# Layer A: two kinds of third score rounds in one PSUM tile, engine orders fixed by keys, products dealt anew

## The chip, the cores and the metric

The kernel runs on one core of a Trainium2 chip. The metric is the device time of one execution in microseconds (us). TensorE is called PE, VectorE DVE, ScalarE ACT, GpSimd POOL and SyncE SP, as in the profile.

## The reference

Four layers, A B A B, act on 2048 tokens of width 640, each as x = x + layer(layernorm(x)). Layer A is attention in 4 segments of 512 tokens with a memory that is carried from segment to segment; 32 heads of 20 columns:

```python
for s in range(N):                      # 4 segments
    logits = jnp.einsum('bhqd,bhkd->bhqk', qs, ks) * scale + mask   # causal
    p = _softmax(logits, axis=-1)
    a_dot = jnp.einsum('bhqk,bhkd->bhqd', p, vs)
    pq = phi(qs)                        # where(t > 0, t + 1, exp(t))
    a_mem = einsum(pq, M) / (einsum(pq, z)[..., None] + 1e-06)
    outs.append(g * a_mem + (1.0 - g) * a_dot)
    pk = phi(ks)
    M, z = M + einsum(pk, vs), z + sum(pk)
return o @ wo
```

Layer B is a recurrent one with 64 steps. The change does not touch it.

## The kernel before

The full kernel builds layer A, layer B, layer A and layer B one after the other. The first layer A reads x as bf16 from the input, the second reads fp32 rows from DRAM.

Layer A works on groups of 4 heads: 8 groups (G = 0 to 7) in each of 4 segments (n = 0 to 3), so g = 8n + G runs from 0 to 31, with two more turns of the loop to drain. A group has two halves, each of which takes one pair of heads. A half has two visits, and after each visit comes one of four slots (0 to 3) with other products.

In a visit two kinds of scores are made. The scores S have the queries on the partitions: only their row maxima are needed (`s_mask` adds the causal mask by a product, `s_mm` multiplies, `s_max` takes maxima on DVE). The turned scores T have the keys on the partitions; the maximum is already added into the queries (`negmax_rows`, `q_with_max`, tile q2), so that `t_round` multiplies and `t_exp` takes the exponential on ACT and then clears the upper triangle on POOL (a select). T runs three halves behind S. Each kind has three rounds for a pair: round 0 is 1024 elements to a partition (two heads with 512 columns), round 1 is 1024 and round 2 is 512. The maxima of round 1 are two instructions, of 768 and 256 elements. "S2" is the third round of S, "exp0" the exponential of the first round of T, and so on; a prime (S2', exp0') marks the second half of a group.

A round has one PSUM tile of two banks, from the pool `psx` with three buffers; `pg` has two buffers of one bank for all other products. Both are rings: a tile takes the buffer of the tile three (or two) places before it and waits until that one has been read. Before, a half takes six tiles, (S0, T0, S2) and (T1, S1, T2), and each visit reuses the buffers of the visit before it.

The other products of a group, by their tiles: QP and qT (the queries of the next group, `proj_q`), EQ, rq and phiq (phi of the queries), KV with Kn and vaug (keys and values, `proj_kv`, in two parts KV0 and KV1), KT and kT (turned keys, `k_turn`), EK and phik (`phi_k`; POOL clips EK between them, called EKm), NUM, nsb, rd and am (the memory's part, `state_num`), UP, upm, MZ and MZb (the memory's update, `state_up`), PV and osb (`pv`), rl, adn and Onat (`norm`). In segment 0 there is no NUM, EQ or phiq, in segment 3 no EK, phik or UP. The layernorm of the next segment is dealt out by `seg_step`: xt is loaded by `seg_load`, `seg_norm` takes statistics on DVE, a power on POOL and xn on DVE, and `seg_tr` turns xn on PE (tps) and copies it to xnT on ACT. The output of the segment before is dealt out by `filler`: `out_stage_a` loads xr and turns Onat (otps, oT), `out_stage_b` multiplies with wo (YP0 and YP1, one for each half of the columns), adds xr (xnew0 and xnew1 on DVE), stores the rows, makes a bf16 copy on POOL (xnb) and stores that. xnew has one buffer of its own in the first layer A, and is the tile xr (two buffers) in the second.

What sets the order: in layer A only PE runs in the order of the code (`_OrdNC` chains each instruction to the one before on its engine, `engines=("tensor",)`). The order on DVE, ACT and POOL is chosen when the program is built, by the scheduler of the language. On the chip each engine runs its own queue in order. Most of layer A's PE instructions carry L101 in the profile, the line of that helper.

Before, G = 2 to 5 of segments 1 to 3 hold an output tile each, and the four layernorm tiles stand in G = 0, 1, 6 and 6. The first layer A also loads layer B's resident weights, 1 MB at a time, from ACT's queue (`load_B_resident`, G = 0 to 4), each behind a small copy on POOL that waits for kT.

Of the kernel before, what the change touches and what calls it, by code (L numbers as in the profile page):

```python
# [18 lines left out]
F32 = mybir.dt.float32  # L19
# [9 lines left out]
D = 640  # L29
# [91 lines left out]

class AWeights:
    pass

# [36 lines left out]
def layer_A(nc, tc, C, W, x_src, x_dst, src_is_bf16, nseg=4, out_bf16=False, xb_dst=None, load_w=None, side_loads=None):  # L161
    SC = 1.0 / math.sqrt(20.0)
    nc_raw = nc
    nc = _OrdNC(tc, nc_raw, engines=("tensor",))
    NGR = 8 * nseg
    KOFF = (0, 640, 1024, 512)
    assert not out_bf16
    with ExitStack() as ctx:
# [65 lines left out]
        def seg_norm(n_, tt):  # L234
            d = SEG[n_]
            xt = d["xt"][tt]
            xn = pxn.tile([128, D], BF16, name="a_xn")
            layernorm_tile(nc, sml, C, xt[:, 0:D], xn[:], "a_ln")
            d["xn"][tt] = xn

        def seg_tr(n_, tt):
            d = SEG[n_]
            if "xnT" not in d:
                d["xnT"] = pxT.tile([128, NCH, 512], BF16, name="a_xnT", tag="xnT")
            xn = d["xn"][tt]
            tps = pg.tile([128, NCH, 128], BF16, name="a_tps", tag="pg")
            for c in range(NCH):
                nc.tensor.transpose(tps[:, c, :], xn[:, 128 * c:128 * c + 128], C.identb[:])
            nc.scalar.copy(d["xnT"][:, :, 128 * tt:128 * tt + 128], tps[:])

        def out_stage_a(n_, tt):
            d = SEG[n_]
            r0 = n_ * 512 + tt * 128
            xr = wkl.tile([128, D], BF16 if src_is_bf16 else F32, name="a_xr")
            nc.sync.dma_start(xr[:], x_src[r0:r0 + 128, :])
            oT = wkl.tile([128, NCH, 128], BF16, name="a_oT")
            d["xr"][tt], d["oT"][tt] = xr, oT
            tps = pg.tile([128, NCH, 128], BF16, name="a_otps", tag="pg")
            for c in range(NCH):
                nc.tensor.transpose(tps[:, c, :], d["Onat"][:, tt, 128 * c:128 * c + 128], C.identb[:])  # L260
            nc.scalar.copy(oT[:], tps[:])

        def out_stage_b(n_, tt, halves=(0, 1)):
# [6 lines left out]
            for half in halves:  # L270
                YP = pg.tile([128, 320], F32, name="a_YP", tag="pg")
                for c in range(NCH):
                    nc.tensor.matmul(YP[:], lhsT=oT[:, c, :], rhs=W.wo[:, c, 320 * half:320 * half + 320],
                                     start=(c == 0), stop=(c == NCH - 1))
                nc.vector.tensor_tensor(out=xnew[:, 320 * half:320 * half + 320], in0=YP[:], in1=xr[:, 320 * half:320 * half + 320], op=ALU.add)
# [4 lines left out]
            nc.gpsimd.tensor_copy(xnb[:], xnew[:])  # L280
# [4 lines left out]
        def proj_q(g):  # L285
# [8 lines left out]
            nc.scalar.copy(qT[:], QP[:])  # L294
            s_["qT"] = qT
            if n >= 1:
                EQ = w1.tile([128, 512], BF16, name="a_EQ")
                nc.scalar.activation(out=EQ[:], in_=QP[:], func=ACT.Exp)
                rq = w1.tile([128, 512], BF16, name="a_rq")
                nc.vector.tensor_scalar(out=rq[:], in0=qT[:], scalar1=0.0, scalar2=None, op0=ALU.max)  # L300
                phiq = wk.tile([128, 512], BF16, name="a_phiq")
                nc.vector.scalar_tensor_tensor(out=phiq[:], in0=EQ[:], scalar=1.0, in1=rq[:], op0=ALU.min, op1=ALU.add)
                s_["phiq"] = phiq

        def proj_kv(g, hf):
# [8 lines left out]
            for dst, o in ((Kn[g % 2], 0), (vaug[g % 4], 80)):  # L314
                nc.scalar.copy(dst[:, 2 * hf:2 * hf + 2, :, 0:20], KV[:, :, o:o + 80].rearrange("p t (j s) -> p t j s", s=20))
            GS[g]["va"] = vaug[g % 4]

        def k_turn(g):
# [4 lines left out]
            nc.scalar.copy(kT[:], KT_[:].rearrange("p t k -> p (t k)"))  # L323
            GS[g]["kT"] = kT

        def phi_k(g):
# [5 lines left out]
            nc.scalar.activation(out=EK[:], in_=KNv, func=ACT.Exp)  # L332
            nc.gpsimd.tensor_scalar(out=EK[:], in0=EK[:], scalar1=1.0, scalar2=0.0, op0=ALU.min, op1=ALU.max)
            pk = phik[g % 2]
            nc.vector.scalar_tensor_tensor(out=pk[:, :, :, 0:20], in0=KNv, scalar=0.0, in1=EK[:], op0=ALU.max, op1=ALU.add)
            GS[g]["pk"] = pk

        def state_num(g):
            n, G = divmod(g, 8)
            s_ = GS[g]  # L340
            if n >= 1:
# [5 lines left out]
                nc.scalar.copy(nsb[:], NUM[:, :, :, 0:21])  # L347
                rd = sm.tile([128, 4, 4], F32, name="a_rd", tag="rd")
                nc.vector.tensor_tensor(out=rd[:], in0=nsb[:, :, :, 20], in1=epsc[:].rearrange("p (a b) -> p a b", a=4), op=ALU.add)
                nc.vector.reciprocal(out=rd[:], in_=rd[:])  # L350
                nc.vector.tensor_tensor(out=rd[:], in0=rd[:], in1=W.g[:, 4 * G:4 * G + 4].unsqueeze(1).to_broadcast([128, 4, 4]), op=ALU.mult)
                am = up.tile([128, 4, 4, 20], F32, name="a_am", tag="am")
                nc.gpsimd.tensor_tensor(out=am[:], in0=nsb[:, :, :, 0:20], in1=rd[:].unsqueeze(3).to_broadcast([128, 4, 4, 20]), op=ALU.mult)
                s_["am"] = am

        def state_up(g):
            n, G = divmod(g, 8)
            s_ = GS[g]
            if n <= nseg - 2:
# [6 lines left out]
                nc.vector.tensor_tensor(out=upm[:], in0=UP[:], in1=C.bdmask[:], op=ALU.mult)  # L366
                nc.gpsimd.tensor_tensor(out=MZ32[:, G, :], in0=MZ32[:, G, :], in1=upm[:], op=ALU.add)
                nc.gpsimd.tensor_copy(MZb[:, G, :], MZ32[:, G, :])
# [27 lines left out]
        def s_max(p, r, X):  # L396
            g, pr = divmod(p, 2)
            nm = GS[g]["nm"]
            for qc, o, w_ in S_SPAN[r][2]:
                nc.vector.tensor_reduce(out=nm[:, qc, 2 * pr:2 * pr + 2], in_=X[:, :, o:o + w_], axis=AX.X, op=ALU.max, negate=True)  # L400

        def negmax_rows(g):
            nm, N_ = GS[g]["nm"], NM[g % 2]
            nc.gpsimd.tensor_copy(N_[:, :, :, 20], nm[:])
            nc.gpsimd.tensor_tensor(out=N_[:, :, :, 21], in0=nm[:], in1=N_[:, :, :, 20], op=ALU.subtract)

        def q_with_max(g):
# [8 lines left out]
            nc.scalar.copy(q2[:], Q2[:])  # L416
# [5 lines left out]
        def t_round(p, r, Y):  # L422
# [7 lines left out]
            for n_, (kc, o, w_) in enumerate(parts):  # L430
                for e in range(2):
                    j = 2 * pr + e
                    rows = slice(32 * j, 32 * j + 32)
                    nc.tensor.matmul(Y[:, e, o:o + w_], lhsT=kT[rows, 128 * kc:128 * kc + 128], rhs=q2[rows, 128 * kc:512],
                                     start=True, stop=True, tile_position=(32 * j, 0), skip_group_check=True)

        def t_exp(p, r, Y):
# [4 lines left out]
            nc.scalar.activation(out=PT[:, :, b:b + width], in_=Y[:, :, 0:width], func=ACT.Exp, scale=SC)  # L442
            dv = PT[:, :, b:b + 128 * diag].rearrange("p e (a q) -> p e a q", q=128)
            nc.gpsimd.affine_select(out=dv, in_=dv, pattern=[[0, 2], [0, diag], [1, 128]], compare_op=ALU.is_ge,  # L444
                                    fill=0.0, base=0, channel_multiplier=-1)

        def pv(g):
# [11 lines left out]
            nc.scalar.copy(osb[:], PV[:, :, :, 0:21])  # L459
            s_["osb"] = osb  # L460

        def norm(g):
# [6 lines left out]
            nc.vector.reciprocal(out=rl[:], in_=osb[:, :, :, 20])  # L469
            nc.vector.tensor_tensor(out=rl[:], in0=rl[:], in1=W.omg[:, 4 * G:4 * G + 4].unsqueeze(1).to_broadcast([128, 4, 4]), op=ALU.mult)  # L470
            Ov = SEG[n]["Onat"][:, :, 80 * G:80 * G + 80].rearrange("p t (j d) -> p t j d", d=20)
            rb = rl[:].unsqueeze(3).to_broadcast([128, 4, 4, 20])
            if n == 0:
                nc.gpsimd.tensor_tensor(out=Ov, in0=osb[:, :, :, 0:20], in1=rb, op=ALU.mult)
            else:
                adn = w1.tile([128, 4, 4, 20], F32, name="a_adn")
                nc.gpsimd.tensor_tensor(out=adn[:], in0=osb[:, :, :, 0:20], in1=rb, op=ALU.mult)
                nc.gpsimd.tensor_tensor(out=Ov, in0=s_["am"][:], in1=adn[:], op=ALU.add)
# [14 lines left out]

        def seg_step(n, G, slot):
            if n + 1 >= nseg:
                return
            for tt, at in enumerate((((0, 0), (0, 2), (0, 3)), ((0, 3), (1, 1), (1, 3)), ((5, 2), (6, 0), (6, 1)), ((6, 0), (6, 2), (6, 3)))):
# [3 lines left out]

        def filler(g, slot):
            n, G = divmod(g, 8)
            out = n >= 1 and 2 <= G <= 5 and n <= nseg
            if slot == 0:
                if 0 <= g - 1 < NGR:
                    state_up(g - 1)
                if g + 1 < NGR:
                    proj_q(g + 1)
            elif slot == 1:  # L510
                if 0 <= g - 1 < NGR:
                    q_with_max(g - 1)
                if g + 1 < NGR:
                    proj_kv(g + 1, 0)
                if out:
                    out_stage_a(n - 1, G - 2)
            elif slot == 2:
                if g < NGR:
                    phi_k(g)
                    state_num(g)  # L520
                if g + 1 < NGR:
                    proj_kv(g + 1, 1)
                if out:
                    out_stage_b(n - 1, G - 2, (0,))
            else:
                if g + 1 < NGR:
                    k_turn(g + 1)
                if 0 <= g - 2 < NGR:
                    pv(g - 2)
                    norm(g - 2)  # L530
                if out:
                    out_stage_b(n - 1, G - 2, (1,))
            seg_step(n, G, slot)

        for g in range(NGR + 2):
            n, G = divmod(g, 8)
            for half in range(2):
                p, tp = 2 * g + half, 2 * g + half - 3
                for ph in range(2):
                    items = ((("S", 0), ("T", 0), ("S", 2)), (("T", 1), ("S", 1), ("T", 2)))[ph]  # L540
                    todo = []
                    for kind, r in items:
                        if kind == "S" and g < NGR:
                            todo.append((kind, p, r, s_mask(p, r)))
                        elif kind == "T" and 0 <= tp < 2 * NGR:
                            todo.append((kind, tp, r, t_tile()))
                    for kind, p_, r, X in todo:
                        (s_mm if kind == "S" else t_round)(p_, r, X)
                        (s_max if kind == "S" else t_exp)(p_, r, X)
# [3 lines left out]
            if side_loads is not None and n == 0:  # L553
                if G == 0:
                    build_gates(nc, st, W, side_loads[1])
                side_loads[0](G, GS[g]["kT"])
        for tt in range(4):
# [670 lines left out]
```

## Time and profile before

| | |
|---|---|
| time of 3 runs | 2785.61, 2791.94, 2794.06 us; median 2791.94 |
| profiled execution | 2787.25 us, span 2785.5 us |
| mean granted clock of PE | 0.981 |
| busy over the span | PE 2574.7 (92%), DVE 1686.6 (61%), ACT 1584.9 (57%), POOL 715.2 (26%) |
| loop of the first layer A, first to fourth segment | windows 30 to 118, 118 to 208, 208 to 296, 296 to 380 us |
| loop of the second | windows 1419 to 1502, 1502 to 1595, 1595 to 1683, 1683 to 1767 us |

The profile's page gives each engine's busy time in 40 equal slices of the span, as digits in tenths. Its timeline lists instructions with start, duration and, in brackets, the idle time before them and what ended it. Durations of neighbours overlap a little: an exponential of 1024 elements lasts 1.02 us, but the next instruction on ACT starts 0.92 us after it. Busy time of PE is modelled in part, so a busy PE need not be the bound.

### The profile page before, as it was taken

How to read it: one execution, taken by the hardware profiler on the slowest of the kernel's cores; microseconds unless marked ns; L12 is line 12 of the kernel's file. 1: busy time of each engine (PE TensorE's matmuls, PEld its weight loads, DVE VectorE, ACT ScalarE, POOL GpSimd, SP SyncE). 2: the span in 40 equal slices, each digit the busy share in tenths (PEclk: the TensorE clock that was granted, in tenths of full speed). 3: DMA queues.
4: the chain of work that ended last, by engine and by line, in shares of the span. 5: the costliest groups of instructions: out<-in, count | busy, mean ns of one | idle time of the engine just before them, and what ended most of it. 6: DMA issues, size and time to landing. Idle time of an engine off the chain costs nothing. (4 is left out here: it accounts for less than half of the span.)

```text
span 2785.5 us, 146956 instructions
## 1 busy us (share of the span) xinstructions
PE 2574.7 (92%) x65414; PEld 1700.1 (61%) x65480; DVE 1686.6 (61%) x4553; ACT 1584.9 (57%) x3708; POOL 715.2 (26%) x1645
## 2 busy tenths in 40 slices
PE   5888879999999999999978888799999999999998
PEld 3555556666666666666645555556666666666665
DVE  6888854555555555555578888445555555555554
ACT  4888854555555555544458888445555455555443
POOL 4666541111111111111146665411111111111110
PEclk9999979999999999999989999899999999999999
DMA  6111162221212212111120111721211121211110
GB/s 239 41 44 40 30 195 69 45 46 41 45 43 45 43 43 45 43 39 30 41 99 28 51 49 37 231 47 39 42 42 40 40 44 40 43 41 38 39 26 20
DMA packets 322300, 156.36 MB, mean 56 GB/s; under 512 B 245760, under 2 KB 310400, under 8 KB 318592
## 3 DMA queue, kind: packets, MB, share of 16 engines
q1 hardware_dynamic: 320224, 136.47, 19.2%
q8 instruction: 512, 8.39, 1.3%
q10 hardware_dynamic: 1440, 10.49, 1.0%
q14 instruction: 124, 1.02, 0.1%
HBM read 95.15 MB, written 51.71 MB: 53 GB/s over the span
## 5 line engine op out<-in xcount | busy, mean ns | idle before, releaser
L101 PEld LDWEIGHTS <-b_HX 128*32 128x32 bf16 x15360 | 430.2, 97 | 341.0 <-issue 14.1
L101 POOL TENSOR_TENSOR b_Pm<-b_E,b_rs 128x96 bf16<-128x96 bf16 x128 | 63.3, 495 | 1443.2 <-ACT b_Vth L101 1094.2
L400 DVE TENSOR_REDUCE a_nm<-a_S 128x2 f32<-128x1024 f32 (+3 forms) x512 | 396.5, 815 | 51.4 <-PE a_T L101 26.6
L442 ACT ACTIVATE a_PT<-a_T 128x1024 bf16<-128x1024 f32 (+1 forms) x384 | 325.4, 889 | 84.9 <-PE a_T L101 50.6
L101 PE MATMUL b_OPS<-b_wo,b_OTsb 128*32 128x320 bf16 x8192 | 308.0, 301 | 10.3 <-issue 8.5
L101 PEld LDWEIGHTS <-b_OTsb 128*32 128x32 bf16 x8192 | 200.5, 97 | 97.0 <-DVE b_OTsb L101 24.1
L101 DVE CAST b_HX<-b_MT 128x8 bf16<-128x8 f32 x372 | 63.7, 172 | 277.5 <-PE b_MT L101 272.2
L444 POOL TENSOR_SCALAR_AFFINE_SELECT a_PT<-a_PT 128x256 bf16<-128x256 bf16 (+1 forms) x384 | 193.5, 520 | 143.2 <-ACT a_PT L442 141.0
L101 ACT CAST b_msb<-b_OPS 128x64 bf16<-128x64 f32 x378 | 69.3, 256 | 237.7 <-PE b_OPS L101 237.7
L101 ACT CAST b_kq<-b_Kb 128x512 bf16<-128x512 f32 x128 | 74.9, 585 | 201.6 <-PE b_Kb L101 201.6
L101 DVE COPY b_KT<-b_TPak 128x128 bf16<-128x128 bf16 x128 | 28.8, 225 | 227.0 <-PE b_TPak L101 227.0
L101 PE MATMUL b_Va<-b_wv,b_HX 128*32 128x512 bf16 x2520 | 160.8, 380 | 0.0
L101 PE MATMUL b_Vb<-b_wv,b_HX 128*32 128x512 bf16 x2520 | 160.1, 379 | 0.0
L101 PEld LDWEIGHTS <-b_kq 128*128 128x128 bf16 x2080 | 116.8, 98 | 68.8 <-ACT b_kq L101 55.6
L101 PE MATMUL b_Ka<-b_wk,b_HX 128*32 128x512 bf16 x2520 | 158.8, 379 | 0.0
L101 DVE TENSOR_SCALAR b_kq<-b_Qa 128x512 bf16<-128x512 f32 x128 | 88.5, 691 | 115.9 <-PE b_Qa L101 112.9
L101 PE MATMUL b_Kb<-b_wk,b_HX 128*32 128x512 bf16 x2520 | 158.6, 379 | 0.0
L101 PE MATMUL b_Qb<-b_wq,b_HX 128*32 128x512 bf16 x2520 | 158.6, 379 | 0.0
L101 PE MATMUL b_Qa<-b_wq,b_HX 128*32 128x512 bf16 x2520 | 158.6, 379 | 0.0
L101 DVE CAST b_OTsb<-b_OTP 128x160 bf16<-128x160 f32 (+1 forms) x384 | 122.3, 374 | 39.6 <-PE b_OTP L101 39.6
L101 PE MATMUL b_vtail<-b_wv,b_TX 128*32 128x256 bf16 x2880 | 137.7, 271 | 6.6 <-issue 3.5
L101 ACT ACTIVATE b_E<-b_SP 128x320 bf16<-128x320 f32 (+1 forms) x256 | 81.1, 368 | 109.0 <-PE b_Va L101 95.3
(195 smaller groups left out, 5764.8 us busy)
## 6 DMA issues: line engine op xcount, KB each, us to landing
b_QKd<-b_tu SPq DMA_DIRECT2D x128, 128.0 KB
b_tl<-b_QKd SPq DMA_DIRECT2D x128, 128.0 KB
b_wv<-in_B_Wv_dram SPq DMA_DIRECT2D x10, 1024.0 KB
b_wo<-in_B_Wo_dram SPq DMA_DIRECT2D x16, 640.0 KB
b_VTd<-b_vt SPq DMA_DIRECT2D x256, 32.0 KB
b_Vth<-b_VTd SPq DMA_DIRECT2D x512, 16.0 KB
b_XO<-xres SPq DMA_DIRECT2D x256, 30.0 KB
b_wk<-in_B_Wk_dram ACTq DMA_DIRECT2D x5, 1024.0 KB
```

Of the source, the lines that this page charges most:

```text
L101: r = f(*a, **k)
L400: nc.vector.tensor_reduce(out=nm[:, qc, 2 * pr:2 * pr + 2], in_=X[:, :, o:o + w_], axis=AX.X, op=ALU.max, negate=True)
L442: nc.scalar.activation(out=PT[:, :, b:b + width], in_=Y[:, :, 0:width], func=ACT.Exp, scale=SC)
L444: nc.gpsimd.affine_select(out=dv, in_=dv, pattern=[[0, 2], [0, diag], [1, 128]], compare_op=ALU.is_ge, fill=0.0, base=0, channel_multiplie ...
```

## The change

All of it is in `layer_A`.

- The third rounds share a tile: "X2" holds S2 of the present pair in columns 0 to 255 of each bank and T2 in columns 256 to 511. T2 now belongs to the pair before that of T0 and T1, so both use the same rows of PE. A half takes five tiles, (X2, T0, S0) and (S1, T1). All products of a visit are issued first, then the maxima and exponentials.
- `KeyOrder` records every instruction of layer A's loop on ACT, DVE and POOL with a key: the number of the visit (4 for each group; 0.3 more in a slot) plus a constant for its kind (`A_LAGS`). At the end each engine's instructions are sorted by key and chained in that order.
- The products between visits are dealt anew (`SLOTS`). Output tiles move from G = 2 to 5 to G = 4 to 7, the layernorms from G = 0, 1, 6, 6 to G = 1, 2, 4, 5 (`TPS`).
- EQ is computed from qT (SBUF) instead of QP (PSUM).
- `layernorm_tile` is written out in `seg_norm` with the same instructions.

```diff
+class KeyOrder:
...
+    def note(self, eng, kind, ins):
+        if self.base is not None:
+            self.n += 1
+            self.rec.setdefault(eng, []).append((self.base + self.lags.get(kind, 0.0), self.n, ins))
+
+    def close(self):
+        for rows in self.rec.values():
+            rows.sort(key=lambda r: r[:2])
+            for a, b in zip(rows, rows[1:]):
+                self.tc.add_manual_dep(b[2], a[2].name, self.info, reason="order")
+        self.rec, self.base = {}, None
...
+A_LAGS = {"EK": 0.3, "EKm": 0.65, "EQ": 1.4, "Kn": -0.1, "MZ": -0.7, "MZb": -0.7, "NM1": -0.2, "On": 3.0,
+          "adn": -0.1, "am": 1.9, "exp0": 0.1, "exp1": -0.1, "exp2": 0.1, "kT": 0.1, "mv": -2.1, "nsb": -0.2,
+          "oT": 0.3, "osb": 0.4, "phik": 2.8, "phiq": 3.5, "pow": -2.1, "q2": 0.5, "qT": 0.2, "rd1": 0.2,
+          "rd2": 0.2, "rd3": 0.2, "rl1": 1.6, "rl2": 1.6, "rq": -0.2, "rs": -2.1, "sel": -0.5, "st": -2.1,
+          "upm": 0.3, "va": 0.2, "xn": 1.0, "xnT": 0.5, "xnb": 2.7, "xnew": 0.6}
...
-            nc.scalar.copy(qT[:], QP[:])
+            K("qT").scalar.copy(qT[:], QP[:])
...
-                nc.scalar.activation(out=EQ[:], in_=QP[:], func=ACT.Exp)
+                K("EQ").scalar.activation(out=EQ[:], in_=qT[:], func=ACT.Exp)
...
-        def t_round(p, r, Y):
+        def t_round(p, r, Y, o0=0):
...
-                    nc.tensor.matmul(Y[:, e, o:o + w_], lhsT=kT[rows, 128 * kc:128 * kc + 128], rhs=q2[rows, 128 * kc:512],
+                    nc.tensor.matmul(Y[:, e, o0 + o:o0 + o + w_], lhsT=kT[rows, 128 * kc:128 * kc + 128], rhs=q2[rows, 128 * kc:512],
...
-            nc.scalar.activation(out=PT[:, :, b:b + width], in_=Y[:, :, 0:width], func=ACT.Exp, scale=SC)
+            K(f"exp{r}").scalar.activation(out=PT[:, :, b:b + width], in_=Y[:, :, o0:o0 + width], func=ACT.Exp, scale=SC)
...
+        TPS = (((0, 0), (1, 3), (2, 1)), ((1, 2), (2, 3), (3, 2)), ((2, 3), (4, 0), (4, 2)), ((4, 0), (5, 1), (5, 3)))
+        SLOTS = (('QP', 'Q2'), ('NUM', 'KV0', 'otps', 'UP'), ('KV1', 'YP0'), ('KT', 'PV', 'YP1'))
+        VISITS = (('X2', 'T0', 'S0'), ('S1', 'T1'))
+        OUT_LAG = 4
...
+        def item(what, g):
+            no, Go = divmod(g - OUT_LAG, 8)
+            out = no >= 1 and Go < 4
+            if what == "UP" and 0 <= g - 1 < NGR:
+                state_up(g - 1)
+            elif what == "QP" and g + 1 < NGR:
+                proj_q(g + 1)
...
+            elif what == "PV" and 0 <= g - 2 < NGR:
+                pv(g - 2)
+                norm(g - 2)
+            elif what == "otps" and out:
+                out_stage_a(no - 1, Go)
+            elif what in ("YP0", "YP1") and out:
+                out_stage_b(no - 1, Go, (int(what[2]),))
+
         def filler(g, slot):
...
+            K.base = 4 * g + slot + 0.3
+            for what in SLOTS[slot]:
+                item(what, g)
+            seg_step(g // 8, g % 8, slot)
...
                 p, tp = 2 * g + half, 2 * g + half - 3
                 for ph in range(2):
-                    items = ((("S", 0), ("T", 0), ("S", 2)), (("T", 1), ("S", 1), ("T", 2)))[ph]
+                    K.base = 4 * g + 2 * half + ph
                     todo = []
...
+                        if kind == "X":
+                            X = s_mask(p, r) if g < NGR else t_tile()
+                            if g < NGR:
+                                todo.append(("S", p, r, X, 0))
+                            if 0 <= tp - 1 < 2 * NGR:
+                                todo.append(("T", tp - 1, r, X, 256))
...
-                    for kind, p_, r, X in todo:
-                        (s_mm if kind == "S" else t_round)(p_, r, X)
-                        (s_max if kind == "S" else t_exp)(p_, r, X)
+                    for step in range(2):
+                        for kind, p_, r, X, o0 in todo:
+                            f = (s_mm, s_max)[step] if kind == "S" else (t_round, t_exp)[step]
+                            f(p_, r, X, *((o0,) if o0 else ()))
```

## The prediction

> **What bounds it now.** First the page's slices: the change touches layer A alone, which fills slices 0 to 5 and 20 to 25 of the 40.
>
> ```profile
> PE   5888879999999999999978888799999999999998
> DVE  6888854555555555555578888445555555555554
> ACT  4888854555555555544458888445555455555443
> ```
>
> No engine is full there: PE, VectorE (DVE) and ScalarE (ACT) all show 8. So the layer is set by waits between engines. Next, windows of one group each, cut at the copies `a_kT<-a_KT` (one per group, called "kT" here; columns: window, length, busy time of PE, PEld, DVE, ACT, POOL): an output group, a plain group of the last segment, and group 1.
>
> ```profile
> 152.49:164.45 11.96, 9.80 (x140) 6.60 (x141) 9.60 (x20) 9.49 (x20) 7.81 (x16) 1.00 0.17 56
> 296.35:305.38 9.03, 8.26 (x123) 5.26 (x122) 7.92 (x16) 8.41 (x17) 5.60 (x12) 1.00 0.11 2
> 30.09:45.12 15.03, 8.93 (x85) 5.45 (x83) 13.69 (x29) 5.74 (x12) 4.83 (x12) 0.89 0.61 231
> ```
>
> A plain group keeps ACT busy 93%, an output group 79%; group 1 is DVE's, with two layernorms packed into it. Last, the timelines at the end of an output group, where the 1.18 us gap arises (start, duration, operation, idle time and releaser):
>
> ```profile
> 240.76 1.51 ACT L442 ACTIVATE a_PT<-a_T 128x1024 bf16<-128x1024 f32 x2 [0.72 <-PE a_S L101]
> 242.16 0.59 ACT L323 COPY a_kT<-a_KT 128x512 bf16<-128x512 bf16 x1
> 242.62 0.47 ACT L459 COPY a_osb<-a_PV 128x336 f32<-128x336 f32 x1
> 244.27 1.02 ACT L442 ACTIVATE a_PT<-a_T 128x1024 bf16<-128x1024 f32 x1 [1.18 <-PE a_T L101]
> ```
>
> ```profile
> 242.80 0.84 PE L101 MATMUL a_YP<-a_wo,a_oT 128*128 128x320 bf16 x5 [0.65 <-ACT a_kT L323]
> 243.48 0.39 PE L101 MATMUL a_S<-c_negu,c_identb 128*128 128x128 bf16 x4
> 243.80 0.39 PE L101 MATMUL a_S<-a_kT,a_qT 32*128 32x512 bf16 x2
> ```
>
> ```profile
> 237.83 1.82 DVE L400 TENSOR_REDUCE a_nm<-a_S 128x2 f32<-128x1024 f32 x2 [1.03 <-PE a_T L101]
> 239.57 0.17 DVE L349 TENSOR_TENSOR a_rd<-a_nsb,a_epsc 128x16 f32<-128x16 f32 x1
> ```
>
> ```profile
> 245.47 0.72 POOL L280 CAST a_xnb<-a_xnew 128x640 bf16<-128x640 f32 x1
> 246.14 0.41 POOL L444 TENSOR_SCALAR_AFFINE_SELECT a_PT<-a_PT 128x256 bf16<-128x256 bf16 x1
> ```
>
> PE waits for kT, does the output product (0.68 us), the masks (0.32), then the scores; ACT waits for all of it. DVE's two maxima run back to back (1.74 to the next start), and POOL (GpSimd) copies the finished rows, xnb, ahead of the next select.
>
> **Unit prices**, start to next start in such rows: exp of 1024 elements 0.92 (its end at 1.02), of 512 0.47; qT 0.48 (end 0.58), q2 0.46, nsb 0.32 (end 0.43), Kn and vaug 0.18 each, EK 0.47, oT and xnT 0.65, kT to its end 0.59. DVE: maxima of r2 0.60 (end 0.68), r0 1.14, r1 1.20; rq 0.33, rl 0.38, rd 0.60, upm 0.20, phiq 0.68, xnew 0.45. Handovers 0.05; a score product of 256 columns to its maximum 0.33, r1's turned scores to their exp 0.43.
>
> **Part by part.** The operations and their sizes stay. EQ reads qT instead of QP: priced as before, hidden by the wait below. What changes is order, and three things bind in the built order.
>
> *The shared tile.* S2 and T2 open each visit, and in the built program the exp of T2 (exp2) waits for DVE's maximum of S2, although the two read different columns. Before, that exp waited for PE alone and ran behind its neighbour (the x2 row at 240.76). Behind exp2 on ACT are exp0, qT and q2, and PE's Q2 and NUM wait for these. So a group begins: end of kT, S2 0.05, maximum 0.33, 0.68, exp2 0.05: **1.11** after kT. With an output product ahead DVE must first do xnew1 (ready 0.91 after YP1's first product starts, 0.44 long), and it is 0.05 + 1.35 + 0.68 + 0.05 = **2.13**. (Before, by the rows above: 244.27 − 242.75 = 1.52.) [...] No run here shows a shared tile yet. By the row at 240.76 alone, without that wait, some 0.6 us (maximum 0.68, less what T2 itself takes) would fall away at each of 64 group heads, about 39 us.
>
> *First half, exp2 to the second exp2 (exp2').* The keys put rq ahead of r1's maxima, and rq needs qT, which ACT does after exp2 and exp0. So DVE stands idle for about 1 us, with rl and r1's maxima queued behind rq and T0's next buffer behind those, and then goes 0.47 + 0.92 + 0.58 + 0.04, rq 0.33, rl 0.38, r1 1.20, rd 0.60, upm 0.20 = 4.72, then r2's maximum and exp2', 0.73: **5.45** (5.25 in segment 3, without upm). In output groups PE is later: nsb ends at 3.68, vaug at 4.13, UP 0.21, masks 0.32, S2' 0.33, then 0.73: **5.72** (5.38 in segment 3, without EK and UP). In segment 0, without rq and rd, the mask after exp1 binds: **4.62**.
>
> *Second half.* exp2' 0.47, exp0' to its end 1.02; T1' reuses T0's buffer, so 0.05 + 0.43 follow; exp1' 0.92, kT 0.59: **3.48**.
>
> A group is the sum: plain 10.04 (segment 3: 9.84; segment 0: 9.21), output 11.33 (segment 3: 10.99). Before: plain 9.03 to 9.6, output 11.96 (11.73). So the fuller head makes plain groups worse and the new deal of products makes output groups better.
>
> *Layer 1 alone:* xnew has one buffer there, and POOL's key order puts the bf16 copy xnb behind the next group's exp0' select. From the second output group on xnew0 waits: exp0' ends 1.49 after exp2', select 0.47, EKm 0.45, xnb 0.72, handover 0.05, xnew0 0.49 = 3.67. PV needs that buffer (1.0), then YP1: the tail and head become 6.80 instead of 5.61, so **+1.19** for 9 groups. Layer 2 writes into the two xr buffers and does not pay. On DVE r1's maxima and xnew1 are queued behind xnew0.
>
> *SP's queue:* the loads of xt and xr move with their steps; each is issued most of a group (9 us or more) before its use, and the stores stay behind the operations that they wait for: nothing, and some 2 us a place if a load were late.
>
> *Layernorm and transposes* (segments 1 and 2): statistics before rd 1.13 in two groups, xn before r1's end 0.37 twice and 0.10, xnT before exp1' 0.65 less 0.22 of waiting, twice, one transpose in the head 0.24: **4.2** a segment. In segment 0 (groups 2 to 7) 2.2, since DVE has slack.
>
> **Sum** (before: from kT start to kT start).
> - Group 1: 15.0 and 14.5 before. Without layernorms in its first half I get 8.4 from DVE's rows; some of it runs at half clock (page row PEclk 9). −6 per layer.
> - Segment 0, groups 2 to 7: 6 × 9.21 + 2.2 = 57.5, against 63.3 and 59.6: −5.8 and −2.1.
> - Segments 1 and 2: 4 × 10.04 + 4 × 11.33 + 4.2 = 89.7, in layer 1 plus 3 × 1.19 = 93.3. Before: 90.4 and 88.2, then 92.5 and 88.7: +2.9, +5.1, −2.8, +1.0.
> - Segment 3, whose output now falls into its last four groups, one of them outside these rows: +1.4 and −0.9.
> - Layer 1: −2.4; layer 2: −10.8. The drain and layer B: nothing moves. **−13 us.**
>
> The profiled execution took 2787.25 (span 2785.5 and 1.75 around it), so 2774; it lies 4.7 under the median of the three runs, 2791.94, and at the median it is 2779. I take **2779**. The span of the three runs is 0.3%, about what can be told from no change.
>
> Costs that no row shows: DVE releasing ACT (I take PE's 0.05; from 0 to 0.2, at 128 places −6 to +19 us); EQ's read from another memory (−0.1 to +0.1 each, hidden: ACT's own queue ends 0.2 to 0.5 before exp2'); the two row groups meeting in X2 (0 to 0.1 us of PE, hidden).
>
> **Rivals.**
> 1. *Slower: DVE's stretch from qT to the second r2 maximum is longer than its lone rows.* All plain and layernorm groups end there. For: the same operation takes longer in other rows (phik 0.49 and 0.91, rq 0.31 to 0.49), and a fixed order cannot step around one late operand. Against: the maxima, two thirds of it, hardly vary. 0.4 us in 64 groups is +26, so 2805. It decides from 0.33 us a group (that is −13 + 21 = +8). Chance 0.21.
> 2. *The early gain does not come:* groups 1 to 7 of segment 0 are held by half clock and by the 1 MB weight loads on ACT's queue, and stay as they were: −13 + 20, of which I count 12 as lost: 2791. Against: in layer 2 no load runs and group 1 is just as long. Chance 0.17.
> 3. *xnb does not hold xnew0,* since POOL is ahead of its key: 9 × 1.19 less, 2768. Against: the built wait is there, and the select before it waits for exp0'. Chance 0.12.
> 4. *The change does not do what it says* (the order is not kept, or T2 gets its own tile): the built program shows five tiles a visit pair and fixed queues. Below 0.01.
>
> **Numbers.** Forecast case 0.50, its own range 2770 to 2790 (the DVE to ACT handover). Rivals 1 to 3 as given. The range 2762 to 2806 leaves out half of rival 1's upper side and little else. Bounds of 0.3% lie at 2783.5 and 2800. Faster: 0.38 of the forecast's 0.50, rival 3's 0.12, 0.02 of rival 2: 0.52. Same: the forecast's other 0.12, 0.13 of rival 2, 0.03 of rival 1: 0.28. Slower: 0.18 of rival 1, 0.02 of rival 2: 0.20.
>
> **What would show it.** In the new trace: ACT's exp2 released by DVE in both halves, 1.1 us after kT in plain groups and 2.1 in output groups; DVE idle about 1 us before rq, released by qT; plain groups near 10.0 and output groups near 11.3, in layer 1 near 12.5 with xnew0 released by POOL's xnb; group 1 near 9. Wrong, if plain groups stay at 9.0 to 9.5 (then DVE was not last), or if output groups lie above 12 in layer 2 (then rival 1, or a wait that I have not seen).

## The result, and the profile after

The changed kernel took 2801.86 us (median of 5 runs, 2800.81 to 2804.04), the kernel before 2791.94 (5 runs, 2785.61 to 2796.79): a ratio of 1.0041 with an interval of 1.0023 to 1.0058. It is slower by 0.4%, where 0.5% faster was forecast. The profiled span went from 2785.5 to 2799.7 us, +14.2.

In layer A's slices 0 to 5 and 20 to 25 no digit of the page differs by more than one tenth from before; ACT is a tenth lower in four of them (2, 3, 4 and 23), and no engine is fuller throughout:

```profile
PE   6888878999999999999978888799999999999998
DVE  7878754555555555555578888545555555555554
ACT  5877754555555555544458878545555455555443
```

Windows of one group each in the new trace (columns as before; the last three are PE's granted clock, the share of the DMA engines and GB/s): group 1 and an output group of the first layer A whose xnew0 waits for xnb ("waiting" here), an output group of the second layer A without that wait, and a plain group of the last segment.

```profile
29.80:38.98 9.18, 7.04 (x75) 4.21 (x73) 8.82 (x16) 4.93 (x10) 2.78 (x9) 1.00 0.80 309
181.72:194.42 12.70, 9.98 (x140) 6.81 (x141) 9.79 (x19) 9.33 (x19) 7.69 (x16) 1.00 0.16 54
1579.15:1590.53 11.38, 9.96 (x146) 6.85 (x144) 10.05 (x20) 9.33 (x19) 7.69 (x16) 1.00 0.25 74
1705.92:1715.99 10.07, 8.38 (x128) 5.36 (x126) 8.35 (x17) 8.29 (x17) 5.86 (x12) 1.00 0.01 2
```

Group 1 fell from 15.03 to 9.18. The output group without the xnb wait fell from 11.96 to 11.38. The plain group rose from 9.03 to 10.07, with ACT now busy 82% of it instead of 93%. The timeline of ACT in that plain group shows where:

```profile
1706.44 0.46 ACT L130 COPY a_osb<-a_PV 128x336 f32<-128x336 f32 x1
1707.76 0.60 ACT L130 ACTIVATE a_PT<-a_S 128x512 bf16<-128x512 f32 x1 [0.86 <-DVE a_nm L130]
1708.25 1.02 ACT L130 ACTIVATE a_PT<-a_T 128x1024 bf16<-128x1024 f32 x1
1709.16 0.59 ACT L130 CAST a_qT<-a_QP 128x512 bf16<-128x512 f32 x1
...
1711.70 0.71 ACT L130 ACTIVATE a_EQ<-a_qT 128x512 bf16<-128x512 bf16 x1
1713.33 0.60 ACT L130 ACTIVATE a_PT<-a_S 128x512 bf16<-128x512 f32 x1 [0.91 <-DVE a_nm L130]
```

`a_PT<-a_S` is exp2 (T2 lies in S2's tile). Twice in this group ACT stands idle for 0.9 us until DVE has the maximum of S2, and exp0, whose tile nobody else reads and whose products on PE ended at 1707.01 and 1712.32, is queued behind it (it starts at 1708.25 and 1713.82). DVE in the same group:

```profile
1707.04 1.82 DVE L130 TENSOR_REDUCE a_nm<-a_S 128x2 f32<-128x512 f32 x2 [0.39 <-PE a_T L101]
1709.78 0.29 DVE L130 TENSOR_SCALAR a_rq<-a_qT 128x512 bf16<-128x512 bf16 x1 [0.93 <-ACT a_qT L130]
...
1712.06 0.63 DVE L130 TENSOR_TENSOR a_rd<-a_rd,a_g 128x16 f32<-128x16 f32 x1
1712.61 1.81 DVE L130 TENSOR_REDUCE a_nm<-a_S 128x2 f32<-128x512 f32 x2
```

It waits 0.93 us for qT, which ACT made late, and the last rd lasts 0.63 us where it took 0.17 before. At the end of the waiting output group, DVE, then POOL, then PE:

```profile
182.18 0.49 DVE L130 TENSOR_TENSOR a_xnew<-a_YP,a_xr 128x320 f32<-128x320 f32 x1 [2.03 <-POOL a_xnb L130]
```

```profile
181.43 0.72 POOL L130 CAST a_xnb<-a_xnew 128x640 bf16<-128x640 f32 x1
```

```profile
182.72 1.15 PE L101 MATMUL a_PV<-a_vaug,a_PT 128*128 128x32 bf16 x40 [1.34 <-DVE a_xnew L130]
183.72 0.84 PE L101 MATMUL a_YP<-a_wo,a_oT 128*128 128x320 bf16 x5
```

The copy of the last output tile, late on POOL, holds xnew0 of this one, xnew0 holds its buffer, and PV on PE waits 1.34 us for it. All the idle time of ACT ahead of the exponentials of layer A, by its releaser (us, times), of the kernel before and then of the changed one:

```profile
  PE a_T L101: 50.6, 69
  PE a_S L101: 31.7, 45
  POOL a_PT L444: 1.5, 2
```

```profile
  DVE a_nm L130: 116.2, 114
  PE a_T L101: 3.0, 4
```

84 us became 119, and nearly all of it is the wait for DVE.

### The profile page after: what moved, and what is told of

Same layout as the page of the kernel before. It is cut to its first block, busy times and chain, and to the rows that moved or that the text cites. A ratio compares the mean times of both kernels' runs of the same rounds, so it can differ in the third digit from the quotient of the medians.

```text
span 2799.7 us, 146921 instructions
## 1 busy us (share of the span) xinstructions
PE 2584.4 (92%) x65418; PEld 1705.2 (61%) x65480; DVE 1697.9 (61%) x4553; ACT 1577.3 (56%) x3708; POOL 707.2 (25%) x1645
## 3 DMA queue, kind: packets, MB, share of 16 engines
q14 instruction: 123, 1.01, 0.1%
## 5 line engine op out<-in xcount | busy, mean ns | idle before, releaser
L101 PEld LDWEIGHTS <-b_HX 128*32 128x32 bf16 x15360 | 428.4, 97 | 343.8 <-issue 14.7
L130 DVE TENSOR_REDUCE a_nm<-a_S 128x2 f32<-128x512 f32 (+3 forms) x512 | 396.2, 816 | 61.4 <-PE a_T L101 33.7
L130 ACT ACTIVATE a_PT<-a_T 128x1024 bf16<-128x1024 f32 (+1 forms) x264 | 270.0, 1032 | 3.4 <-PE a_T L101 3.0
```

The lines of the kernel that those rows point to most:

```text
L101: r = f(*a, **k)
L130: r = f(*a, **k)
```

## The experiments

They ran on three chips (e1 to e4, e5 to e8, e10 to e13), each time beside the kernel before, which took 2783.25, 2782.22 and 2784.42 us there. The changed kernel itself was not run again beside them. So all are compared by their ratio to the kernel before; by its ratio of 1.0041 the changed kernel would take about 2795 there, which is an estimate, and "under the changed kernel" means the difference of the two ratios. Each edit is to the changed kernel unless another is named.

**e1, xnb early.**

```diff
- "xnb": 2.7
+ "xnb": 0.1
```

> Edit: the key constant of xnb goes from 2.7 to 0.1, so that POOL copies the finished rows before the selects of the next group instead of behind three of them. Theory (xnb holds xnew0 in the first layer A): the seven groups there that wait (14.35, 12.70, 13.66, 14.33, 13.82, 13.70 and 11.97 us in the trace of the changed kernel) come down to those of the second layer A (11.67, 11.38, 11.25, 11.66, 11.39, 11.24, 11.14), so 14.8 us less: about 2787. Rival (those groups are long for another reason, such as PE running slower or the first layer's weight loads): the wait of xnew0 on xnb goes, but groups stay above 12.5 and the time within 5 us of 2802.

Measured: 2778.15, ratio 0.9980 (0.9969 to 0.9990), 17 us under the changed kernel. The seven groups came to 11.66, 11.39, 11.31, 11.66, 11.39, 11.31 and 11.14 us, 14.7 less together. The theory holds. The trace of the changed kernel shows beside it why most of those groups cost more than the 1.19 us forecast: two of the seven (12.70 and 11.97) ran at full clock, the other five at a mean granted clock of 0.88, as these windows show (the clock is the third column from the end):

```profile
169.40:171.00 1.60, 1.60 (x15) 1.02 (x12) 0.77 (x3) 0.44 (x1) 1.33 (x3) 0.50 0.00 0
...
266.01:280.34 14.33, 11.80 (x145) 7.82 (x146) 9.80 (x19) 10.03 (x21) 7.71 (x16) 0.88 0.14 47
280.34:294.16 13.82, 11.23 (x140) 7.33 (x141) 9.80 (x19) 9.33 (x19) 7.69 (x16) 0.88 0.15 49
```

The first is inside such a group, just after PE had stood idle for 1.34 us: PE ran at half clock there. (That the clock makes up the rest was not tried by itself.)

**e2, rq later.**

```diff
- "rq": -0.2
+ "rq": 0.9
```

> Edit: the key constant of rq goes from -0.2 to 0.9, so that DVE does rl and round 1's two maxima before it turns to rq, instead of standing idle for qT with them queued behind. Theory A (DVE's fixed order from rq to the second r2 maximum sets the first half of a group): the idle time of 0.53 to 0.94 us before rq goes in the 47 groups that have an rq, 25 to 44 us less: 2758 to 2777, and plain groups of the last segment come down from 10.1 to 9.2 to 9.6. Theory B (the head is set by the shared tile, and behind it PE and ACT are as late as DVE): DVE stands idle for round 1's scores instead, and the time falls by less than 8 us.

Measured: 2777.73, ratio 0.9979 (0.9966 to 0.9991), 17 us under the changed kernel: between the theories. The wait before rq is gone (it was 30.6 us at 46 places), but in its stead DVE stands idle 1.28 us before round 1's maxima, released by PE, and plain groups of the last segment fell only from 10.08 to 9.78. So DVE's order was one late thing among others that are equally late.

**e3, rd later.**

```diff
- "rd1": 0.2, "rd2": 0.2, "rd3": 0.2
+ "rd1": 1.0, "rd2": 1.0, "rd3": 1.0
```

> Edit: the key constants of the three rd instructions go from 0.2 to 1.0, behind the maxima of the next visit. Theory A (DVE's stretch ahead of the second r2 maximum is the last to end, and rd lasts 1.05 in it instead of the 0.60 I had counted, since its last instruction is stretched beside POOL): 0.6 to 1.05 us less in 48 groups, so 29 to 50 us less: 2752 to 2773. Theory B (the second exp2 is held by ACT's or PE's own work as well): less than 8 us. If only the stretch by POOL's neighbouring work matters, rd's last instruction is back at 0.17 and 0.46 in 48 groups, 22 us, are gained.

Measured: 2778.72, ratio 0.9987 (0.9975 to 0.9998), 15 us under the changed kernel: again between the theories. The durations of rd (ns, least, median, most) in the changed kernel and then in e3:

```profile
L130 DVE RECIPROCAL a_rd<-a_rd x48: 252/253/254, 104.8 to 1765.1; 128x16 f32<-128x16 f32 x48
L130 DVE TENSOR_TENSOR a_rd<-a_rd,a_g x48: 174/606/635, 105.0 to 1765.4; 128x16 f32<-128x16 f32 x48
```

```profile
L130 DVE TENSOR_TENSOR a_rd<-a_rd,a_g x48: 174/174/178, 110.0 to 1752.6; 128x16 f32<-128x16 f32 x48
```

The stretch of 0.43 us is real and went away; but PE then let DVE wait 0.71 us before the second r2 maximum.

**e4, T2 in its own tile again.**

```diff
- VISITS = (('X2', 'T0', 'S0'), ('S1', 'T1'))
+ VISITS = (('S2', 'T0', 'S0'), ('S1', 'T1', 'T2'))
```

> Edit: T2 gets a tile of its own again and stays with the pair of T0 and T1; the visits are (S2, T0, S0) and (S1, T1, T2), keys and deal stay. Theory B (the shared tile makes exp2 wait for DVE at 128 places, 0.73 us each, of which the head of a group and of its second half pay): ACT's first exponential of a half no longer waits for DVE; with 0.5 to 0.7 us at 64 to 128 places, 32 to 60 us less: 2742 to 2770. Theory A (DVE's fixed order is the bound): exp0 and qT come 0.7 us earlier, so the wait before rq shrinks, but what it gains DVE's stretch still needs; 0 to 20 us less. Rival C (six tiles in three buffers make each visit wait for the one before, as in the kernel before): no gain, 2790 to 2810.

Measured: 2736.69, ratio 0.9832 (0.9810 to 0.9854), 58 us under the changed kernel and 47 under the kernel before. Theory B holds, and at the top of what it expected: plain groups of the last segment take 8.96 us, with ACT busy for 8.49 of it. But this edit moves T2 as well as taking the wait away.

**e7, the shared tile kept, exp2 behind exp0.**

```diff
- "exp2": 0.1
+ "exp2": 0.15
```

> Edit: the tile stays shared; only the key constant of exp2 goes from 0.1 to 0.15, so that ACT does exp0 first and exp2 behind it, while DVE takes S2's maximum. The changed kernel would read about 2795 beside a kernel before of 2783, as on the chip of the last runs. Theory 1 (the loss is ACT's wait for DVE's S2 maximum at the head of each half): exp2's wait of 0.7 us at 128 places goes behind exp0's 0.92 us, ACT's gaps before exp2 (0.9 to 1.2) shrink to what T0 needs, and of the 58 us that the separate tile of e4 brought, 35 or more come back: 2760 or less. Theory 2 (the ring of five tiles in three buffers: PE's masks for S0' wait for S1's maximum, those for S1' for exp2): exp2 ends later than now, PE's masks wait longer, and the time stays within 10 us of 2795 or is longer.

Measured: 2743.18, ratio 0.9858 (0.9841 to 0.9875): 51 us under the changed kernel by the order of two instructions on ACT. Theory 1 holds. Plain groups of the last segment went from 10.08 to 8.73. ACT at the head of one of them, and then its idle time ahead of exp2 over the whole kernel:

```profile
1665.28 1.02 ACT L130 ACTIVATE a_PT<-a_T 128x1024 bf16<-128x1024 f32 x1 [0.24 <-PE a_T L101]
1666.20 0.59 ACT L130 ACTIVATE a_PT<-a_S 128x512 bf16<-128x512 f32 x1
1666.67 0.59 ACT L130 CAST a_qT<-a_QP 128x512 bf16<-128x512 f32 x1
```

```profile
  DVE a_nm L130: 9.7, 18
```

While ACT does exp0, DVE takes S2's maximum, and exp2 mostly finds it done: 116 us of waiting for DVE became 10. All the idle time of ACT ahead of the exponentials fell from 119 to 56 us; 39 of it is now for PE.

**e5, no keys.**

```diff
- for rows in self.rec.values():
+ for rows in ():
```

(in `close`, so that nothing is chained)

> Edit: the tile stays shared and the products lie as in the change, but the keys are not applied: the scheduler chooses the order on DVE, ACT and POOL as it did before. Theory 1 (the shared tile is the loss, the fixed order is not): the built order still makes exp2 wait for DVE, 2785 to 2805. Theory 2 (the fixed order with one late operand, rq's qT, is what costs): DVE's idle time before rq goes and 20 to 40 us with it: 2755 to 2775.

Measured: 2751.20, ratio 0.9887 (0.9868 to 0.9906), 43 us under the changed kernel. Theory 1 fell. Theory 2 came near in size (4 us below its range) but had the reason wrong: rq waits only 8.2 us in all, mostly 0.22 us at a time, because the scheduler puts exp0 ahead of exp2 by itself:

```profile
1660.74 1.02 ACT L130 ACTIVATE a_PT<-a_T 128x1024 bf16<-128x1024 f32 x1 [0.24 <-PE a_T L101]
1661.66 0.59 ACT L130 ACTIVATE a_PT<-a_S 128x512 bf16<-128x512 f32 x1
```

So it was the keys that put exp2 first: both have 0.1, and at equal keys the one recorded first goes first.

**e6, the new places alone** (e4 and e5 together: no keys, no shared tile).

```diff
- VISITS = (('X2', 'T0', 'S0'), ('S1', 'T1'))
+ VISITS = (('S2', 'T0', 'S0'), ('S1', 'T1', 'T2'))
...
- for rows in self.rec.values():
+ for rows in ():
```

> Edit: neither keys nor a shared tile; what is left of the change is the new place of the products, output tiles and layernorms, and EQ from qT. Theory 1 (of the 46 us by which e4 beats the kernel before, the new place gives most; group 1 alone is worth 12): 2740 to 2760. Theory 2 (the keys give most of it): 2765 to 2785. I hold it for likelier that both are needed, 2755.

Measured: 2768.24, ratio 0.9945 (0.9931 to 0.9960), 15 us under the kernel before. Theory 2 holds, my own guess of 2755 does not: with their own tiles, the keys add 32 us to what the places bring (e4 against e6), though beside the shared tile they took 43 away (the changed kernel against e5).

**e8, e4 with xnb early and YP1 ahead of PV.**

```diff
- "xnb": 2.7
+ "xnb": 0.1
...
- ('KT', 'PV', 'YP1')
+ ('KT', 'YP1', 'PV')
```

> Edit on e4 (own tile for T2, keys, new places): xnb's key constant 0.1, and YP1 ahead of PV in the last slot, so that PE makes the second output product while ACT copies kT, instead of standing idle 0.70 us for kT with YP1 behind it. In e4 ACT then stood idle 1.14 us before exp0. Expected: ACT's gap at the 24 output groups of both layers falls by 0.6 to 0.9 us, 15 to 20 us, and in the first layer xnb 0.3 us in 6 groups: 2716 to 2722 beside e4's 2737. Rival (PV comes later by 0.7 and osb behind it holds exp0 on ACT as long as YP1 did): no change, 2733 to 2740.

Measured: 2742.47, ratio 0.9848 (0.9831 to 0.9865), no gain over e4, as the rival said, but for another reason: PV's tile is then the buffer of KT, and PE waits for kT's copy all the same (0.69 and 1.01 us before PV). Output groups are 0.3 us longer than in e4 (11.57 against 11.24).

**e10, both edits of e7 and e1.**

```diff
- "exp2": 0.1, "xnb": 2.7
+ "exp2": 0.15, "xnb": 0.1
```

> Edit: the changed kernel with two key constants altered, exp2 0.15 (as e7) and xnb 0.1 (as e1). In e7 the seven groups of the first layer A that wait for xnb are 17.1 us longer than the same groups of the second (12.53, 13.19, 12.77, 12.53, 13.52, 12.88, 12.80 against 10.84, 10.57, 9.97, 10.85, 10.56, 9.90, 10.45). Theory (the two losses are separate and add): 2743 - 17 = 2726, 2720 to 2730. Rival (xnb ahead of the next selects holds them, now that a group is shorter, and gives back part): 2732 to 2742.

Measured: 2723.66, ratio 0.9789 (0.9770 to 0.9809), 2.1% under the kernel before. The theory holds: e7 less 20 us. The seven groups have the second layer's lengths (10.85, 10.56, 9.97, 10.84, 10.57, 9.97, 10.46).

**e11, e4 with xnb early.**

```diff
- "xnb": 2.7
+ "xnb": 0.1
```

> Edit: e4 (own tile for T2) with xnb 0.1, for a comparison with e10 in which both are rid of xnb. e4's groups that wait are 2.2 us longer than the second layer's, so 2735. Theory (a shared tile in the right order is a gain by itself: in the second layer e7's rows are 8.5 us shorter than e4's): e10 lies 9 to 17 us below this run. Rival (sharing is worth nothing): both within 5 us.

Measured: 2733.73, ratio 0.9829 (0.9809 to 0.9849). e10 lies 10 us below, in the range expected; the intervals only just touch. So sharing the tile, with the move of T2 that comes with it, is a gain of some 0.4%, once the order is right.

**e12, e10 with the edits of e2 and e3.**

```diff
- "rq": -0.2, "rd1": 0.2, "rd2": 0.2, "rd3": 0.2
+ "rq": 0.9, "rd1": 1.0, "rd2": 1.0, "rd3": 1.0
```

> Edit: e10 with rq 0.9 and the three rd 1.0, the edits of e2 and e3. Theory 1 (rq and rd only cost 17 and 16 us because exp2 stood ahead of exp0 and made qT late; with exp2 behind exp0 DVE stands idle 0.23 us before rq, and ACT is busy throughout): within 5 us of e10. Theory 2 (DVE's fixed order is a bound of its own): another 15 to 33 us, 2693 to 2711.

Measured: 2723.42, ratio 0.9791 (0.9772 to 0.9810), the same as e10. Theory 1 holds: rq and rd cost time only as long as exp2 stood ahead of exp0.

**e13, e10 with one transpose a slot later.**

```diff
- ((2, 3), (4, 0), (4, 2))
+ ((2, 3), (4, 0), (4, 3))
```

> Edit: e10 with the transpose of the third layernorm tile moved by one slot, from (4, 2) to (4, 3), behind PV and YP1. There are four such places; ACT waits 0.53 us for tps there and S1' is behind it on PE. If tps holds S1': 0.5 to 1 us at 4 places, 2 to 4 us less than e10. If it costs as much at the head of the next group (0.27 of PE, 0.6 of ACT): no change.

Measured: 2720.81, ratio 0.9778 (0.9761 to 0.9796), the lowest of all. The 3 us under e10 are within both intervals. In the rows the group itself fell from 11.37 to 10.86 and the next rose from 11.10 to 11.39, so of the expected gain less than half is seen there; the rest stays open.

## Why the prediction was wrong

The step that failed is the sum of the group lengths, together with what was put at nothing. By the rows the sum came out 27 us too low (-13 against +14): about 15 us in the groups, which are longer than their parts as added up, 5 in the groups that wait for xnb, and 7 in all that lies outside the rows, which was held not to move. The wait that binds, exp2 for DVE's maximum, was read rightly.

Measured as the forecast was made, from kT to kT, in us after less before (first layer A, second):

| stretch | forecast | measured |
|---|---|---|
| group 1 | -6, -6 | -5.8, -6.4 |
| segment 0, groups 2 to 7 | -5.8, -2.1 | -3.7, -1.1 |
| segment 1 | +2.9, -2.8 | +5.5, -0.3 |
| segment 2 | +5.1, +1.0 | +11.6, +5.3 |
| segment 3 | +1.4, -0.9 | +2.9, -0.4 |
| all else | 0 | +6.8 in all |
| sum | -13 | +14 |

- *The shared tile: right in mechanism, too small in price, and wrong in where it comes from.* The built wait of exp2 on DVE's maximum was read rightly and is the cause of the loss: e7 leaves the tile and takes the loss away. (X2 opens the first visit of each half, not each visit, as the prediction once says.) The prediction priced its absence at 39 us, one wait of some 0.6 us at each of 64 heads. With the wait covered (e7) 51 us came back, 1.35 in a plain group, because the second half's exp2' waits as well (0.91 in the group shown). And it was taken for a property of sharing. It belongs to the order: exp2 could stand behind exp0. In the trace of e7 exp2 still waits for that maximum, at 18 of its 120 places, and this costs 10 us instead of 116. (No run has a shared tile without the wait, so what that would do is not shown.)
- *The groups: most parts a little too short.* The head of a plain group took 1.21 us from kT's end (forecast 1.11), since the S2 maximum starts 0.43 after S2's first product instead of 0.33; an output head took 2.21 (2.13), and 2.48 with a transpose of the layernorm in it. The first half took 5.57 in segment 3 (5.25), mostly since rd lasts 1.05 on DVE instead of 0.60, its last instruction 0.63 instead of 0.17. In the plain group of segment 1 it took 5.71 (5.45), and there rd is short (0.58): phik, 0.41 on DVE between rq and rl, was left out of the sum. In output groups it took 5.88 (5.72). The second half was shorter, 3.30 (3.48). Plain groups came to 10.07 and 10.22 instead of 9.84 and 10.04, output groups without a layernorm to 11.24 and 11.39 instead of 11.33 (segment 3: 11.14 instead of 10.99). At least half of the 15 us lies in the groups that hold a layernorm: G = 1 to 5 of segments 1 and 2 took 57.9 to 59.8 us, against 57.0 in the sum (3 × 10.04, 2 × 11.33 and 4.2). In G = 5, for one, a layernorm's statistics run on DVE between kT and the S2 maximum, and the head took 3.03 us; the sum had no such term.
- *xnb: the mechanism right, the size not.* Nine waits came, as forecast, seven of them in the rows. These seven groups cost 14.8 us more than the second layer's, where the sum had 9.5 in the rows (8 × 1.19); e1 gives 17 for all, forecast 10.7. At full clock such a group was 12.70 against 12.52 forecast; the half clock (0.50) behind PE's idle time of 1.34 us was missing from the sum.
- *DVE idle before rq:* forecast 1 us, measured mostly 0.53 to 0.94, released by qT as said. Its queue was held to set the first half. e12 shows that it is no bound of its own.
- *Group 1:* right to 0.4 us in both layers, and rival 2 fell with it.
- *"The drain and layer B: nothing moves"* was wrong: all that lies outside the rows grew by 6.8 us, 3.9 of it behind the last kT of the second layer. There DVE waits for a load of xr, 1.94 us before and 5.85 now:

```profile
1795.70 0.89 DVE L130 TENSOR_TENSOR a_xr<-a_YP,a_xr 128x320 f32<-128x320 f32 x2 [5.85 <-DMA a_xr<-xres]
```

  The last output tile of segment 2 now sits in the last group, just ahead of the drain's four, and xr has two buffers. But e1 keeps that place, and there the time behind the last kT is 1037.8 us, against 1041.1 in the changed kernel and 1037.3 before, with no such wait above 1.5 us. So the place alone does not do it, and the cause stays open.
- *Rivals.* Rival 1 gave 2805, its sign was right, and its reason was part of it: DVE's stretch did grow (by the rd, 0.45 us in segment 3), and taking rd or rq out of it (e2, e3) brought 15 to 17 us each. But it is no bound of its own: the same edits brought nothing once exp2 was moved (e12). Rival 3 fell with e1's result. What the list lacked is the case that decided: that the keys choose a worse order than the scheduler did.

## What to carry to other kernels

When a change brings a new wait and a fixed order together, look at what is queued behind the waiting instruction and whether something that is ready could go first: here the order of two exponentials with equal keys was worth 51 us, five times what the change lost. Price such a wait at every place where it stands, not once a period. A shared buffer and a fixed order are two changes: run each without the other (here +11 together, -31, -47 and -15 us for sharing alone, keys alone and neither, by the ratios to the kernel before, all with the new places), since the sign of either depended on the other.

## What the runs showed of the hardware

- DVE's `a_rd<-a_rd,a_g` took 0.17 us alone. At 28 of its 48 places in the changed kernel it began while one of POOL's selects still had 0.58 us or more to go; there it took 0.60 to 0.64 and ended 0.02 to 0.03 after the select, as in the plain group shown (1712.69, the selects at 1712.67). The sum ahead of it, `a_rd<-a_nsb,a_epsc`, did the same at six places (0.43 to 0.60) and took 0.17 or 0.18 at the others. At four places the select had only 0.15 to go, and the product took 0.17 or 0.18. The reciprocal between kept its 0.25 in all 48 places, at 28 of them beside a select from start to end, and the maxima hardly varied: 0.41 to 0.42 us for 256 elements, 0.67 to 0.69 for 512, 0.94 to 0.96 for 768 and 1.21 to 1.22 for 1024. Why the one stretches beside a select and the others do not is not shown.
- PE fell to a granted clock of 0.50 after 1.34 us of standing idle (with 0.40 shortly before), at 167.0 to 168.4 us; after the same idle time at 181.4 to 182.7 it did not (1.00 over that group). Such a gap of 1.34 or 1.35 us was followed by the lower clock at five of six places. In this trace the 37 changes of the clock all lie whole multiples of 3.41 us apart, and the windows below are laid on that spacing (third figure: busy time of PE; third from the end: its clock):

```profile
165.50:168.91 3.41, 1.66 (x37) 1.14 (x36) 1.73 (x4) 2.50 (x5) 2.92 (x6) 1.00 0.24 73
168.91:172.33 3.42, 3.42 (x47) 2.39 (x43) 1.69 (x4) 1.13 (x2) 1.85 (x4) 0.50 0.08 28
179.15:182.57 3.42, 1.83 (x22) 1.12 (x20) 1.39 (x2) 3.20 (x6) 2.38 (x6) 1.00 0.00 0
```

  At the five places PE was idle for 1.74 or 1.75 us of such a window, and the next had a clock of 0.50; at the sixth the gap lies in two windows, and PE was idle for 1.59 and 0.20 us of them. Elsewhere the clock also fell after less (1.04 us of idle time in the window before 131.37 us), so what brings it down stays open.
